# Feature-major query tiles in a linear-attention kernel: four instead of eight, with a new instruction order

## The chip, the cores and the metric

The kernel runs on one core of one Trainium2 chip. The metric is device time in microseconds of one execution. The core has five engines with a program of their own each: TensorE (matmuls, called PE in the profile), VectorE (DVE), ScalarE (ACT), GpSimd (POOL) and SyncE (SP), which here only issues DMA transfers. Engines wait for each other by semaphores.

## The reference

The input x has 2048 rows (tokens) of 512 features. Four layers change it in turn: attention A, feed-forward B, attention A and feed-forward B, each with the same weights in both of its places. Each layer normalizes x (layernorm without weights), computes, and adds its result to x.

```python
# A: linear attention, 32 heads of 16 features
q, k, v = split(layernorm(x) @ wqkv)
pq, pk = q @ w_phi, k @ w_phi                      # per head
phi_q = concat(softmax(pq), softmax(-pq))          # 32 features per head
phi_k = concat(softmax(pk), softmax(-pk))
kv, z = sum_s phi_k[s] v[s], sum_s phi_k[s]        # over all tokens
o = (phi_q @ kv) / (phi_q @ z + 1e-6)
x = x + o @ wo
# B: ReGLU feed-forward, 1376 hidden features
x = x + (relu(y @ W_gate) * (y @ W_up)) @ W_down   # y = layernorm(x)
```

## The kernel before, in words

The tokens are cut into 16 tiles of 128 rows. x stays in SBUF (`x_sb`) in bf16. Of each tile the kernel needs two layouts: tokens on partitions (for softmax sums and residuals) and features on partitions (as an operand of TensorE). The turn from one to the other is a transposing DMA on SP's queue (`dma_tr`, L443), or for tiles 0 and 1, in places where latency counts, a transpose on TensorE with a copy out of PSUM (`pe_tr`, L693).

At the start w_phi is multiplied into the key and query weights (`compose_k`, `compose_q`), so one projection gives pk or pq. The first attention is called A0, the first feed-forward B1, the second attention A2 and the second feed-forward B3; L0 to L3 are the layernorms ahead of them.

Keys and values: `kv_proj` and `kv_pair` project a tile, ScalarE takes the exponentials of pk and -pk, `knorm` (L741) sums them over each head's 16 features (Zk), takes the reciprocal (rZk) and scales (phik, on GpSimd or VectorE). `kv_acc` adds the tile to the sums kv and z in PSUM banks 0 and 1. When all 16 tiles are in, `kv_fin` (L792) copies the sums, masked to blocks, into `kvbd` (68 columns per group of heads) and, in A0 alone, into `kvf` (144 columns, L808).

Queries are done in one of two ways.

- Token-major: `q_proj` (L816) projects a tile with tokens on partitions; ScalarE takes the two exponentials (L827, L831). `qnorm` (L843) does on VectorE the sums Zq (L847) and the reciprocal rZq (L851), then on VectorE or GpSimd the ratio rho (L852), and in two halves the scaling phiq (L855), each half followed by a transposing DMA on SP into `qT` (qtr, L858). `num` (L915) multiplies the transposed tile by `kvbd` in eight matmuls of 68 columns (L921). VectorE divides: rden (L927) and o (L928). `qT` has four buffers.
- Feature-major: `q_fm` (L861) projects four tiles at once with features on partitions, so no transposing DMA is needed. `num_fm` (L874) multiplies the exponentials, not normalized, by `kvf` in eight matmuls of 144 columns (L886); eight of the columns give each softmax's own sum. Three copies take the result out of PSUM (numcp, L413 by way of `evac`, on ScalarE or VectorE), small operations put the two softmax sums together (zm L897, zd L900, zr L901, ab L902), VectorE scales (tsc, L906), and the two halves are added (o, L911, on VectorE or GpSimd). `kvf`, zm, ab and zd's neighbours lie in `qT` buffers 0 and 1, the results of numcp and tsc in tiles of `expk` that are no longer needed.

Both end in `out_proj` (L933): o is transposed (otr), multiplied by wo, and added to x (resid, L687). `center` (L700) then subtracts the mean (apply, L703), transposes the tile into `yT` (L1 tr, L697 or L708) and computes the scale (var L710, vx L712, rx L714).

In the kernel before, A0 has tiles 0 and 1 token-major, tiles 2 to 9 feature-major in two groups of four, and tiles 10 to 15 token-major. A2 is token-major throughout.

The feed-forward (`glu_up`, L947, `glu_down`, L1002) takes tiles 0, 1, then 2 and 3 together, then four at a time. For each of eleven pieces of the hidden features it computes gate and up in PSUM (L962), takes relu on ScalarE (L964) and the product on VectorE (h, L972 or L975). The last piece is short, done in token-major form (gu, L988) and transposed by DMA (htr, L995). `glu_down` multiplies by W_down (L1011).

The order of the work is not that of the calls. `emit` (L1026) emits some 3,960 operations, numbered in the order in which they are emitted. The table `ORDER` (L13) lists for each engine, as base-36 numbers, the operations in the order in which this engine runs them; a search done beforehand wrote it. `CHOICE` (L377) names the engine of each operation that two engines can do. `Program.schedule` replays the lists with assumed durations, and `prepare` derives the semaphore waits. An engine runs its list strictly in order, so a waiting instruction holds everything behind it in its list; on SP these are the transposing DMAs and the weight transfers.

Of the kernel before, what the change touches and what calls it, by code (L numbers as in the profile page):

```python
# [14 lines left out]
        "29 26 6 25 27 28 2a 2b 4t 2c 39 49 3u 4y 4e 44 5i 5n 58 5s 4j 6j 6k 67 73 72 8l 6d 84 6a 4o 83 8k 91 9x 9y 7r 96 9z c4 c5 9b c6 9g d9 da db b4 f9 f8 "  # L15
        "fm fl ay ee ef b2 eg gz gy fz h0 hx hw fy ij g5 g4 ik gb ga gg gh ii hv mk mj n4 n3 mu mt lm lq lt ne nd nn no nt r8 o5 o4 rf of op oq jv kn p0 pa pb "
        "vg pl pw pv vk q6 qg qh qr s1 ko sd sc sn xw xt sx sy t8 lg tt tj ti zn u4 ue u3 zu up uo uz wd wo wp x9 wz xa m8 ru ym yn xk z7 11o z8 yx 10k 11s zi "
        "10l 11v 10v 142 w2 12t yb 149 146 134 13p 135 13f 109 159 14z 13q 15a 15u 12a 15v 15k 14o 16x 178 177 17i 1b7 16m 18l 1aw 1c9 1db 1ad 1by 1d0 1e6 1dv "
        "1ea 1f0 1fg 1ew 1em 1gj 1fw 1gk 1fc 1gi 1jm 1hk 1hl 1hj 1kb 1fs 1ib 1ic 1kr 1l7 1g8 1ia 1j2 1j3 1gx 1ll 1lk 1j1 1m9 1ma 1nv 1k6 1ob 1mz 1my 1lj 1or "
        "1l3 1kn 1p7 1nn 1m8 1mn 1no 1mx 1pl 1pk 1ly 1q9 1nm 1o7 1nc 1qa 1pj 1qz 1qy 1on 1rq 1rp 1q8 1s4 1p3 1qx 1s3 1py 1ro 1t5 1t6 1s5 1s6 1t8 1qn 1t7 1u7 "  # L20
        "1ua 1u8 1xr 1uw 1uv 1u9 1xx 1y3 1uy 1ym 1yn 1ux 1z1 1z2 1y9 1yl 1zh 1zg 1z0 1zv 1zw 1zf 24t 1zu 24u 255 24v 24w 256 258 230 257 25u 25t 25h 25i 25k "
        "25w 25v 25j 26q 271 27d 272 22j 27n 27c 27z 27o 27y 289 28a 28l 28k 28v 28w 297 29h 296 29i 29t 29s 2be 23c 23x 2bp 2bq 24i 2cc 2cb 2c1 26f 2c0 2dj "
        "2cn 2cm 2di 2dt 2b3 2e5 2du 2e4 2ef 2eg 2er 2eq 2ft 2fu 2hu 2i5 2i6 2ih 2ig 2j2 2ir 2j3 2a7 2is 2d7 2kg 2k6 2kh 2k5 2l2 2l3 2ks 2kr 2mh 2le 2mg 2ld "
        "2fi 2hb 2ju 2m5 2qa 2pz 2qb 2n8 2ql 2qw 2qx 2qm 2sa 2r7 2sl 2sb 2r8 2ny 2sw 2sx 2t7 2sm 2pg 2t8 2um 2tj 2ti 2ul 2g8 2rz 2mv 2ua 2vw 2x5 2ak 2v0 2xg "
        "2xr 2xh 2od 2y3 2xs 2y2 2vd 2yd 2yp 2ye 2yo 2z0 2zb 2yz 2zm 2za 2zl 2gl 2wo 2zw 2zx 308 2wb 307 30z 2oq 31c 30m 322 "),
    "dve": (
        "2z 30 33 3a 3b 3e 3l 3m 3v 3k 3w 3p 2m 53 3z 5d 5x 5z 5t 5v 5u 60 5y 5w 7i 7g 7f 7h 6l 64 6m ao 74 ap 75 an am 85 7t 86 8m a0 7x 8n 7v a3 a1 a4 c7 ca "
        "c8 cb dc df b0 fa dg fn dd fo fb eh ek el ei em h1 h2 fq h4 hy hz h5 i1 il im i0 in io j2 j1 j3 j4 ix jd iz je iy j0 k6 jj k7 ku ky l1 l2 jo l3 l4 jp "
        "l6 l7 lv lw ju kc ly lz nu kh rc rg ki rh og ld ri o6 le or p1 rk pc pm rl vn vo q7 m5 px vq qi m6 xp qs kp s2 vs so se r4 sz xy xz t9 rr tk tu y1 u5 "
        "uf uq zr 13s we lh v0 zw zx zy zz rs vc 13t vz x0 wq w0 y8 y9 xb yo xl 13v 106 107 17w yy 15x zj 15y m9 z9 17x 15z 10m 17y 1b9 1ba 19o 10w 12u 11y 181 "  # L30
        "19p 14c 120 121 136 118 14d 13g 16c 14e 16d 150 19r 1cb 127 11k 13r 15b w3 128 1cc 18b 18c 15w 15l 1cd 14l 14m 16y 16j 16k 17j 179 17v 18i 18j 1a3 1a4 "
        "1bo 1bp 19b 1cq 1cr 18z 1aa 1ab 1b8 1dl 1ax 1dm 19n 1bv 1cx 1bw 1cy 1ca 1e8 1ds 1dt 1e7 1eb 1dc 1ey 1fe 1f3 1fh 1d1 1en 1ex 1jk 1kp 1fu 1fx 1gl 1fj "
        "1ft 12b 1k9 1fd 1l8 1ks 1gy 1dw 1hm 1g9 1hn 1j4 1j5 1gm 1id 1ha 1go 1nt 1l5 1nw 1mb 1ie 1i1 1hp 1mc 1la 1o9 1is 1k7 1jj 1p5 1oc 1gn 1os 1op 1ko 1p8 "
        "1lm 1ln 1n0 1ig 1n1 1n2 1l4 1lo 1pm 1lz 1lp 1nd 1np 1mo 1j7 1nq 1pn 1po 1r0 1pp 1r1 1o8 1r3 1qb 1qc 1s7 1s8 1oo 1p4 1rr 1rs 1se 1sf 1pz 1qo 1t9 1tg "
        "1rf 1xp 1ta 1th 1qe 201 1xs 1sw 1xv 202 203 20f 1xu 1ty 1tl 204 20g 1y1 208 209 1yo 1um 1y7 1y6 1yp 1z3 1ya 1yq 1z4 1yc 1zi 1zj 1zl 1zx 1zy 200 1zz "
        "20a 21r 21q 21s 21p 20d 221 222 227 22u 22v 22c 23n 23o 22d 20m 22i 248 249 235 236 265 23b 20n 2et 26r 266 2gm 2eu 24f 23u 23v 273 2ev 27e 2gn 280 "
        "28b 27p 2at 24g 2au 28m 2go 2lg 298 2cx 29j 28x 29u 2cy 2j5 26c 2j6 26d 2n9 2na 2f8 2f9 2bf 23d 2a6 2lh 2br 2aj 2li 2ll 2b0 2h1 2cd 2c2 2h2 2d4 2ff "
        "2co 23y 2b1 2or 2os 2dk 2nc 2d5 2fg 2e6 2eh 2dv 2es 2tl 2fv 2jk 2jl 2g7 2ra 2ou 2b4 2hv 2rb 2i7 2ow 2lv 2tm 2lw 2gk 2it 2h8 2h9 2ii 2j4 2no 2m2 2k7 "
        "2np 2rf 2m3 2jr 2js 2l4 2ki 2kt 2p6 2p7 2lf 2mi 2mu 2rp 2nv 2nw 2rq 2n7 2m6 2u0 2u1 2qc 2q0 2hc 2jv 2op 2oc 2vm 2pd 2qn 2qy 2pe 2r9 2sc 2rw 2rx 2vn "
        "2t9 2sn 2sy 2tk 2un 2uz 2u7 2u8 2vt 2vu 2vc 2x6 2xt 2ub 2xi 2wa 2yf 2wn 2y4 2yq 2s0 2zn 2z1 2zy 2zc 309 30l 30y 31b 31o 320 "),  # L40
    "pool": (
        "2p 0 1 4 2t 5 2w 2x 31 2 2u 2n 2o 32 3c 34 3d 3n 3o 2y 3x 3y 3f 2s 2r 2q 2v 61 62 66 63 69 6c 3 7j 7l 7k 7m 7n 7o 6n 7p 7q 76 ar aq as au at 87 av aw "
        "ax 8o a2 a5 c9 cc dh fp fc de fd ff ej h3 fs en h6 l5 lu lx rj jw vp jx vr vt xx kq y0 zv y2 100 13u 13x 17z li 11w rv 160 11x 14a 14b ma 162 19q 1bb "
        "1be 11z 10a yc 19t 14f 1bc yd 1cg rw w4 1ce 10b 18m 14p 1ec 16n 1ed 1f1 1f2 1fi 1fy 1fz 1jn 1kc 1kd 1bz 18n 16o 1ke 14q 1jo 1kt 1jp 1c0 1ku 1l9 1ae "
        "1ho 12c 1nx 1p9 1dx 1pa 1if 1od 1md 1ny 1oe 1ot 1j6 1d2 1ou 1me 1n3 1af 1r2 1nr 1ns 1sg 1sj 1s9 1sc 1rt 1qd 1sa 1tb 1te 1tc 1xt 206 1sh 1ti 1tj 20h "
        "1y4 1y5 20k 1xy 1xz 1y0 1ru 1yr 1yb 1z6 1z5 1zk 20i 20b 20o 20r 20p 2ew 2gr 2gp 22k 22l 2ey 2j7 2j8 23e 26g 2ja 24j 2nb 24k 23z 2lj 2ot 2b5 2tn 2to "
        "2tq 2d8 26h 2ne 2rc 2rd 2d9 2hd 2fj 2fk 2nz 2o0 2jw 2vx 2ph 2m7 2s1 2pi 2uc 2vy "),
    "pe": (
        "7 8 9 a b c d e f g h i j k 4p 4q 4r 4s l m n o p q r s t u v w x y z 35 36 37 38 10 11 12 13 14 15 16 17 3g 3h 3i 3j 18 45 46 47 48 3q 3r 3s 3t 4z 50 "
        "51 52 59 5a 5b 5c 4u 4v 4w 4x 4a 4b 4c 4d 40 41 42 43 5e 5f 5g 5h 4f 4g 4h 4i 5j 5k 5l 5m 19 1a 1b 54 55 56 57 1c 1d 1e 5o 5p 5q 5r 1f 1g 6f 6g 6h 6i "  # L50
        "1h 6y 6z 70 71 1i 1j 1k 1l 1m 1n 1o 8g 8h 8i 8j 1p 1q 1r 1s 6p 1t 1u 7z 80 81 82 1v 1w 6o 1x 1y 1z 20 21 22 23 24 4k 4l 4m 4n 9l 9m 9n 9o 8x 8y 8z 90 "
        "9h 9i 9j 9k 9p 9q 9r 9s 9t 9u 9v 9w 6q 6r 6s 6t 77 78 79 7a 92 93 94 95 bo bp bq br bs bt bu bv 6u 6v 6w 6x 97 98 99 9a 88 89 8a 8b bw bx by bz c0 c1 "
        "c2 c3 ct cu cv cw 9c 9d 9e 9f cx cy cz d0 d1 d2 d3 d4 d5 d6 d7 d8 f4 f5 f6 f7 fh fi fj fk 7b 7c 7d 7e 8c 8d 8e 8f 8p 8q 8r 8s dy dz e0 e1 a6 a7 a8 a9 "
        "e6 e7 e8 e9 e2 e3 e4 e5 ea eb ec ed fu fv fw fx ae af ag ah cd ce cf cg cl cm cn co 8t 8u 8v 8w aa ab ac ad gm gn go gp gi gj gk gl ai aj ak al ch ci "
        "cj ck gq gr gs gt gu gv gw gx di dj dk dl g0 g1 g2 g3 hn ho hp hq dq dr ds dt ia ib ic id cp cq cr cs dm dn do dp hr hs ht hu g6 g7 g8 g9 du dv dw dx "
        "es et eu ev eo ep eq er gc gd ge gf ie if ig ih mb mc md me mf mg mh mi f0 f1 f2 f3 ew ex ey ez h7 h8 h9 ha hf hg hh hi i2 i3 i4 i5 ip iq ir is hb hc "
        "hd he hj hk hl hm i6 i7 i8 i9 it iu iv iw j5 j6 j7 j8 j9 ja jb jc mz n0 n1 n2 mv mw mx my k2 k3 k4 k5 jf jg jh ji jy jz k0 k1 ml mm mn mo mp mq mr ms "
        "kr ks kt kv kw kx kz l0 jk jl jm jn lj lk ll ln n5 n6 n7 n8 lo lp lr ls n9 na nb nc nf ng nh ni nj nk nl nm jq jr js jt k8 k9 ka kb r5 r6 r7 r9 np nq "
        "nr ns kd ke kf kg ob oc od oe o0 o1 o2 o3 nw nx ny nz ra rb rd re o7 o8 o9 oa ol om on oo oh oi oj ok l9 la lb lc os ot ou ov kj kk kl km p6 p7 p8 p9 "
        "p2 p3 p4 p5 vd ve vf vh ow ox oy oz m1 m2 m3 m4 pr ps pt pu pd pe pf pg pn po pp pq ph pi pj pk vi vj vl vm py pz q0 q1 q8 q9 qa qb q2 q3 q4 q5 qc qd "  # L60
        "qe qf qj qk ql qm xm xn xo xq rx ry rz s0 qn qo qp qq qt qu qv qw qx qy qz r0 r1 r2 r3 s8 s9 sa sb s4 s5 s6 s7 sf sg sh si xr xs xu xv sj sk sl sm sp "
# [354 lines left out]
class Kernel:  # L416
# [609 lines left out]
    def emit(self):  # L1026
# [45 lines left out]
        for li in (0, 2):  # L1072
# [46 lines left out]
            if not last:  # L1119
                self.q_fm(F0 + 4, qring, A, 2)  # L1120
# [93 lines left out]
```

The softmax here doesn't subtract the row's maximum and nothing guards it: scores larger than these inputs give would overflow.

## Time and profile before

| | before |
|---|---|
| median of 3 runs | 379.43 us (379.27 to 379.86) |
| the profiled execution | 379.55 us timed, span 377.4 us |
| TensorE matmul busy | 367.7 us (97%), 2519 instructions |
| VectorE busy | 276.2 us (73%), 607 |
| ScalarE busy | 227.0 us (60%), 463 |
| GpSimd busy | 130.8 us (35%), 234 |
| granted TensorE clock | 1.000 |

The span is from the first to the last instruction of the profiled execution. Busy shares are averages over stages: keys and values of A0 last until about 53 us, B1 and the rest of A0's queries until about 150, B1 with A2's keys until about 236, and then come A2's queries and B3. A line of the groups reads: line of the kernel, engine, operation, output and inputs, shapes, count, then busy us and mean ns of one, then the idle time of the engine just before them and what ended it. A line of the timeline reads: start in us, duration, engine, line, operation, and in brackets how long the engine had been idle and what released it. Matmuls are pipelined, and their recorded durations overlap.

### The profile page before, as it was taken

What the parts mean: (1) busy time and instruction counts of PE and PEld (TensorE: products, weight loads), DVE (VectorE), ACT (ScalarE), POOL (GpSimd) and SP (SyncE); (2) the same over time, 40 slices, a digit from 0 to 9 for tenths busy, and PEclk for the clock granted to TensorE, in tenths of its full rate; (3) what the DMA queues carried; (4) which work ended last, traced back from release to release, by engine and by line L of the source; (5) the groups of instructions that cost most, each with busy time, mean ns of one, the idle gap of its engine ahead of it and who ended that gap; (6) DMA issues with size and microseconds to landing.
All of it is one profiled execution on the core that took longest, in us unless ns stands there. A gap on an engine that the chain in (4) does not pass through costs nothing.

```text
span 377.4 us, 6882 instructions
## 1 busy us (share of the span) xinstructions
PE 367.7 (97%) x2519; PEld 203.9 (54%) x2565; DVE 276.2 (73%) x607; ACT 227.0 (60%) x463; POOL 130.8 (35%) x234
## 2 busy tenths in 40 slices
PE   6999999999999999999999999999999999999997
PEld 5654555877744454454444446577664454445443
DVE  5999998989968676459799999898984654342323
ACT  3999878765744127874677568584635451653450
POOL 6799941133344001350463577023221201000020
PEclk9999999999999999999999999999999999999999
DMA  7632794313326444310300045335543442142012
GB/s 233 173 76 52 187 240 149 77 33 56 78 43 94 97 64 84 70 30 14 70 2 1 2 81 95 79 63 95 83 83 75 81 86 56 28 71 70 30 42 70
DMA packets 87856, 29.33 MB, mean 78 GB/s; under 512 B 79792, under 2 KB 86800, under 8 KB 87824
## 3 DMA queue, kind: packets, MB, share of 16 engines
q1 hardware_dynamic: 84368, 25.86, 33.7%
q10 hardware_dynamic: 3456, 3.05, 2.5%
q8 instruction: 20, 0.33, 0.4%
q14 instruction: 12, 0.10, 0.1%
HBM read 7.91 MB, written 2.10 MB: 27 GB/s over the span
## 4 chain that ended last, share of the span: by engine, by line
PE 85%; POOL 7%; DVE 3%; issue 2%; ACT 1%; DMA 1%; POOLq 0%; DVEq 0%
PE ps L962 37%; PE ps L1011 20%; PE ps L725 7%; PE ps L942 7%; POOL expk L750 5%; PE ps L822 5%; PE ps L988 3%; PE ps L921 2%; PE ps L787 1%; PE ps L886 1%; DMA hT<-in_A_wqkv_dram 1%; DVE Zk L744 1%; POOL rstd L648 1%; PE ps L868 1%; PE ps L539 0%
## 5 line engine op out<-in xcount | busy, mean ns | idle before, releaser
L962 PE MATMUL ps<-yT,Wgu 128*128 128x512 bf16 (+2 forms) x870 | 150.8, 320 | 0.6
L962 PEld LDWEIGHTS ps<-yT,Wgu 128*128 128x128 bf16 x880 | 78.5, 98 | 58.8 <-ACT expk L970 1.0
L964 ACT ACTIVATE gate_sb<-ps 128x512 bf16<-128x512 f32 (+2 forms) x110 | 50.7, 480 | 55.1 <-PE ps L962 41.8
L1011 PE MATMUL ps<-Wd,hT 128*128 128x512 bf16 (+4 forms) x354 | 79.3, 373 | 0.5
L1011 PEld LDWEIGHTS ps<-Wd,hT 128*128 128x128 bf16 (+1 forms) x363 | 34.6, 98 | 39.5 <-DVE hT L972 0.7
L972 DVE TENSOR_TENSOR hT<-gate_sb,expk 128x512 bf16<-128x512 bf16 (+2 forms) x70 | 23.9, 361 | 30.4 <-ACT expk L970 21.4
L970 ACT ACTIVATE expk<-ps 128x512 bf16<-128x512 f32 (+2 forms) x70 | 32.0, 475 | 22.2 <-PE ps L962 19.5
L710 ACT ACTIVATE sq<-x_sb,nmr 128x512 bf16<-128x512 bf16 x48 | 34.6, 721 | 10.3 <-DVE x_sb L687 6.6
L744 DVE TENSOR_REDUCE Zk<-expk 128x64 f32<-128x1024 bf16 x32 | 38.1, 1203 | 1.0 <-ACT expk L737 0.7
L714 POOL TENSOR_TENSOR rstd<-rv,mone 128x1 f32<-128x1 f32 x32 | 18.6, 589 | 50.2 <-DVE rv L712 50.0
L1013 DVE SCALAR_TENSOR_TENSOR x_sb<-ps,rstd,x_sb 128x512 bf16<-128x512 f32 (+2 forms) x33 | 23.9, 728 | 16.1 <-PE ps L1011 13.5
L942 PE MATMUL ps<-wo_p,oT 128*128 128x512 bf16 x118 | 30.8, 379 | 0.6 <-DVE oT L413 0.3
L975 DVE TENSOR_TENSOR hT<-gate_sb,ps 128x512 bf16<-128x512 bf16 (+2 forms) x40 | 21.7, 544 | 12.6 <-ACT gate_sb L964 6.4
L855 POOL TENSOR_TENSOR expq<-expq,rho 128x256 bf16<-128x256 bf16 x36 | 22.2, 624 | 24.4 <-DVE rho L852 23.7
L847 DVE TENSOR_REDUCE Zq<-expq 128x64 f32<-128x1024 bf16 x24 | 28.8, 1204 | 0.8 <-POOL rho L852 0.5
L687 DVE SCALAR_TENSOR_TENSOR x_sb<-ps,x_sb 128x512 bf16<-128x512 f32 x32 | 21.9, 687 | 8.6 <-PE ps L942 7.8
L750 POOL TENSOR_TENSOR expk<-expk,rZk 128x1024 bf16<-128x1024 bf16 x13 | 25.9, 2005 | 0.6 <-DVE rZk L746 0.6
L755 POOL TENSOR_TENSOR expk<-expk,rZk 128x512 bf16<-128x512 bf16 x17 | 19.1, 1134 | 11.8 <-DVE rZk L746 11.5
L822 PE MATMUL ps<-Wqp,yT 128*128 128x512 bf16 x91 | 22.8, 379 | 0.3
L725 PE MATMUL ps<-Wkp,yT 128*128 128x512 bf16 x84 | 22.0, 379 | 0.2
L725 PE MATMUL ps<-wv_p,yT 128*128 128x512 bf16 x85 | 21.9, 379 | 0.2
L712 POOL TENSOR_SCALAR rv<-rv 128x1 f32<-128x1 f32 x22 | 4.3, 203 | 45.3 <-ACT sq L710 45.3
(126 smaller groups left out, 514.1 us busy)
## 6 DMA issues: line engine op xcount, KB each, us to landing
out_dram<-x_sb ACTq DMA_DIRECT2D x15, 128.0 KB, 1.7
x_sb<-in_A_x_dram SPq DMA_DIRECT2D x3, 512.0 KB, 5.0
Wgu<-in_B_W_up_dram SPq DMA_DIRECT2D x4, 344.0 KB, 5.5
Wgu<-in_B_W_gate_dram SPq DMA_DIRECT2D x4, 344.0 KB, 4.3
Wd<-in_B_W_down_dram SPq DMA_DIRECT2D x5, 256.0 KB, 3.3
yT<-ytile SPq DMA_TRANSPOSE x56, 2.5
qT<-expq SPq DMA_TRANSPOSE x40, 2.5
x_sb<-in_A_x_dram SPq DMA_DIRECT2D x4, 128.0 KB, 3.6
```

The lines of the kernel that those rows point to most:

```text
L710: op("act", lambda e: e.activation(k.sq[:], k.x_sb[:, t, :], ACT.Square, scale=-float(D), bias=k.nmr[:, t, :], accum_out=k.rv1[:, t, :]), ...
L725: op("pe", (lambda ic, bank, W: lambda e: e.matmul(k.pb[bank][:], k.yT[:, ic, t * 128:(t + 1) * 128], W[:, ic, :], start=(ic == 0), stop=( ...
L744: op("dve", lambda e: e.tensor_reduce(k.Zk[:, zb, :], k.expk[:, t, :, :, :].rearrange("p g s (h f) -> p (g s h) f", f=16), AX.X, ALU.add), ...
L750: op("pool", lambda e: e.tensor_tensor(kv, kv, k.rZk[:, rb, :].unsqueeze(2).to_broadcast([P, 64, 16]), ALU.mult), [r("expk", t, 0), r("exp ...
L822: op("pe", (lambda ic, bank, tt: lambda e: e.matmul(k.pb[bank][:], k.yT[:, ic, tt * 128:(tt + 1) * 128], k.Wqp[:, ic, :], start=(ic == 0), ...
L847: op("dve", lambda e: e.tensor_reduce(k.Zq[:, b, :], k.expq[:, t, :, :, :].rearrange("p g s (h f) -> p (g s h) f", f=16), AX.X, ALU.add), ...
L942: op("pe", (lambda c, bank: lambda e: e.matmul(k.pb[bank][:], k.oT[:, ob, c, :], k.wo_p[:, c, :], start=(c == 0), stop=(c == NC - 1)))(c, ...
L962: op("pe", (lambda bank, W, ic, fc, Mf: lambda e: e.matmul(k.pb[bank][0:Mf, 0:n], W[:, ic, fc * 128:fc * 128 + Mf], k.yT[:, ic, c0:c0 + n] ...
L964: op("act", (lambda Mf, gb, gs: lambda e: e.activation(k.gate_sb[0:Mf, gs, 0:n], k.pb[gb][0:Mf, 0:n], ACT.Relu))(Mf, gb, gs), [self.RP[gb] ...
L970: op("act", (lambda Mf, ub, up: lambda e: e.activation(up[0:Mf, 0:n], k.pb[ub][0:Mf, 0:n], ACT.Copy))(Mf, ub, up), [self.RP[ub]], ru, 170 ...
L972: op("dve", (lambda Mf, up, gs, u: lambda e: e.tensor_tensor(k.hT[0:Mf, u, 0:n], k.gate_sb[0:Mf, gs, 0:n], up[0:Mf, 0:n], ALU.mult))(Mf, u ...
L1011: op("pe", (lambda fc, Kf, u, c0, bank, m0, m1: lambda e: e.matmul(k.pb[bank][:, m0:m1], k.hT[0:Kf, u, c0:c0 + 128], k.Wd[0:Kf, fc, m0:m1] ...
```

## The change

In A0 only tiles 2 to 5 are feature-major; tiles 6 to 9 become token-major like 10 to 15. The constant F1 = 6 marks the first tile after the feature-major ones; `N` uses it to decide whether a tile goes to `num_fm` or `num`, and from which tile on `qnorm` is called one tile ahead. The second `q_fm` call goes, and `q_proj` runs over the pairs from tile 6 on. The activation table's assumed duration in the planner and the alternatives that the planner knows for L0's centring change as well. ORDER and CHOICE are replaced by those of a new search, for all engines and the whole kernel.

```diff
 F0 = 2
+F1 = F0 + 4
...
-        op("act", ... ACT.Exp), [r("ones")], [r("sq"), r("tbl")], 1450, "table")
+        op("act", ... ACT.Exp), [r("ones")], [r("sq"), r("tbl")], 250, "table")
...
-            self.op2("act" if on_act else "dve", apply, dep, dst, {"dve": 407, "act": 825}, f"{tag} apply {t}", 250.0)
+            how = CHOICE.get(f"{tag} apply {t}", "act" if on_act else "dve")
+            other = "act" if how == "dve" else "pool" if t < 9 and how == "act" else "dve" if how == "act" else "act"
+            dd = {"dve": 407, "act": 825, "pool": 2090}
+            self.op2(how, apply, dep, dst, {e: dd[e] for e in (how, other)}, f"{tag} apply {t}", 250.0)
...
-        tb = (t + 2) % 4 if tag == "A0" and t < F0 else t % 4
+        tb = (t + 2) % 4 if tag == "A0" and (t < F0 or F1 % 4 == 2 and False) else t % 4
...
-                    if (F0 + 7 if li == 0 else 7) <= t < NT - 1:
+                    if (F1 - 1 if li == 0 else 7) <= t < NT - 1:
                         self.qnorm(t + 1, A)
-                    if li == 0 and F0 <= t < F0 + 8:
+                    if li == 0 and F0 <= t < F1:
                         self.num_fm(t, nring, wring, A)
...
-            if not last:
-                self.q_fm(F0 + 4, qring, A, 2)
-            for t in range(F0 + 8 if li == 0 else 8, NT, 2):
+            for t in range(F1 if li == 0 else 8, NT, 2):
                 self.q_proj([t, t + 1] if t < NT - 1 else [t], qring, A, last)
```

In the new lists, as far as the stages around the change go: at the start ScalarE copies yT of tile 1 before that of tile 2 and the V of tile 0, tile 0's copy goes to VectorE, and VectorE centres tile 1 behind the statistics of tiles 2 and 3. GpSimd takes the rstd of tiles 8 to 11 before the first phik. Behind `kv_fin` VectorE copies numerator 2 before oT of tile 0, and does Zq of tile 6 before it scales tile 2. On SP the query transposes stand so: otr 2, a weight, otr 3, htr 0, qtr 6 (two), otr 4, L1 tr 2 and 3, otr 5, qtr 7 (two), htr 1, otr 6, otr 7, L1 tr 5 and 4, qtr 8 (two), L1 tr 6 and 7, htr 2, qtr 9 (two), qtr 12, 11 and 10 (one half each), otr 8. Of the eight phiq of tiles 6 to 9, VectorE does 6 1, 7 0, 9 0 and 9 1, GpSimd the others. Zm, zd, o and numcp of tiles 2 to 5 are divided anew between VectorE, ScalarE and GpSimd.

## The prediction

> **What bounds the kernel now.** I read four views in this order: busy time by stretch, the timeline of the places where TensorE pauses, the timeline of the two matmul forms that the change exchanges, and the groups by line. The first view decides most. Its columns are the stretch in us, its length, then busy time with the number of instructions for TensorE matmuls, weight loads, VectorE, ScalarE and GpSimd, and the granted clock, DMA share and GB/s.
>
> ```profile
> 0.00:20.00 20.00, 16.47 (x149) 11.48 (x152) 15.05 (x34) 13.28 (x23) 14.93 (x45) 1.00 0.68 197
> 20.00:52.00 32.00, 31.73 (x236) 16.37 (x240) 31.73 (x45) 30.36 (x45) 30.83 (x29) 1.00 0.59 119
> 52.00:67.00 15.00, 13.81 (x129) 8.04 (x128) 13.16 (x31) 10.99 (x15) 1.50 (x3) 1.00 0.58 186
> 67.00:110.00 43.00, 42.63 (x410) 31.16 (x415) 36.43 (x103) 26.86 (x84) 13.86 (x31) 1.00 0.27 56
> 110.00:220.00 110.00, 109.42 (x560) 51.87 (x570) 85.52 (x175) 63.86 (x124) 37.44 (x65) 1.00 0.28 50
> 220.00:247.00 27.00, 26.48 (x259) 14.88 (x261) 24.48 (x52) 19.89 (x36) 12.35 (x19) 1.00 0.43 83
> 247.00:372.00 125.00, 124.21 (x766) 68.26 (x780) 68.14 (x170) 61.78 (x141) 19.88 (x43) 1.00 0.33 64
> ```
>
> Busy matmul time overlaps itself and proves little, so I priced the work by the interval at which matmuls follow each other in dense places: 216 ns for 512 columns (47 in 10 us in the dense feed-forward), 109 for 256, 83 for 192, 56 for 128, 62.5 for 144, about 32 for 68. Counting the weight loads of each stretch by form, TensorE's own work is 31.6 of the 32 us from 20 to 52, 12.6 of 15 from 52 to 67, 43.0 of 43, 109.8 of 110, 25.8 of 27, and 125 of 125. TensorE idles only in the start (about 10 us, filled with warm-up matmuls), 2.4 us between 52 and 67, 1.2 us between 220 and 247, and at the tail. Elsewhere a nanosecond taken from TensorE is a nanosecond of span, and a wait put ahead of a matmul in its program order is one too. From 20 to 52 VectorE is as full (31.7 of 32).
>
> The pauses of the second kind, on VectorE (first fence) and TensorE (second), around the change from keys and values to queries:
>
> ```profile
> 57.62 0.69 DVE L928 TENSOR_TENSOR osb<-ps,rden 128x512 bf16<-128x512 f32 x1
> 59.10 1.49 DVE L413 CAST expk<-ps 128x432 bf16<-128x432 f32 x3 [0.79 <-PE ps L886]
> 62.58 1.23 DVE L906 TENSOR_TENSOR expk<-expk,qT 128x1024 bf16<-128x1024 bf16 x1 [0.25 <-POOL qT L902]
> 65.14 0.43 DVE L413 COPY yT<-ps 128x512 bf16<-128x512 bf16 x1 [0.38 <-PE ps L697]
> ```
>
> ```profile
> 59.77 0.30 PE L886 MATMUL ps<-qT,expq 128*128 128x144 bf16 x2 [0.52 <-DVE expk L413]
> 65.72 0.64 PE L988 MATMUL ps<-Wgu,yT 128*128 128x192 bf16 x4
> ```
>
> The feed-forward starts at 65.72, as soon as VectorE has copied yT of tile 0 out of PSUM (65.14). This copy is the gate of the stage.
>
> **What the Trainium skill says.** "TensorE: Matmul & The Clock Gate", Back-to-back issue gap, gives N/2.4 + 2.5 ns for an isolated gap and about 81 ns sustained at 128 columns with weight loads. Only the first agrees here: four 144-column matmuls take 0.25 us (77.89 to 78.14, 62.5 each; the formula gives 62.5), eight of 68 columns 0.25 us (243.82 to 244.07, 31 each; 30.8).
>
> ```profile
> 77.89 0.41 PE L886 MATMUL ps<-qT,expq 128*128 128x144 bf16 x4
> 78.14 1.28 PE L962 MATMUL ps<-yT,Wgu 128*128 128x128 bf16 x20
> 243.82 0.42 PE L921 MATMUL ps<-kvbd,qT 128*128 128x68 bf16 x8
> 244.07 1.02 PE L822 MATMUL ps<-Wqp,yT 128*128 128x512 bf16 x4
> ```
>
> "Perfetto Trace Analysis", Identifying the Most-Contended Engine, warns that matmul busy share is no measure; the trace agrees (97% busy, yet 10 us of it warm-up and gaps at the start). "DMA: Bandwidth & Descriptors", DMA Transpose (X-bar), lets only the SP and ACT queues carry plain transposes, so each added one is a turn of SP here; the trace shows 1.19 to 1.27 us per issue and 2.5 us to landing.
>
> **The change part by part.** Edits that emit nothing new cost 0: the activation table's assumed duration, the second-choice engine of the centring (the engines chosen are those of before), the q_buf condition that ends in `and False`. Tiles 6 to 9 leave the feature-major path. TensorE's projection is the same: 16 matmuls of 512 columns and four exponentials of 1.02 us on ScalarE, in the same places and PSUM banks.
>
> Numerator. 32 matmuls of 144 columns become 32 of 68: 32 x (62.5 - 31) = 1.0 us less TensorE work, all in the full stretch after 67. It counts whole.
>
> Vector-like work. The rows:
>
> ```profile
> L847 DVE TENSOR_REDUCE Zq<-expq 128x64 f32<-128x1024 bf16 x24 | 28.8, 1204 | 0.8 <-POOL rho L852 0.5 <-ACT expq L827 0.2
> L906 DVE TENSOR_TENSOR expk<-expk,qT 128x1024 bf16<-128x1024 bf16 x8 | 9.7, 1213 | 2.6 <-POOL qT L902 2.6
> L928 DVE TENSOR_TENSOR osb<-ps,rden 128x512 bf16<-128x512 f32 x24 | 16.5, 687 | 0.9 <-DMA oT<-osb 0.2
> L413 ACT ACTIVATE expk<-ps 128x432 bf16<-128x432 f32 x11 | 5.9, 535 | 1.6 <-PE ps L886 1.6
> L855 POOL TENSOR_TENSOR expq<-expq,rho 128x256 bf16<-128x256 bf16 x36 | 22.2, 624 | 24.4 <-DVE rho L852 23.7
> ```
>
> A tile loses tsc (1.21) and zr (0.35) on VectorE and gains Zq 1.20, rZq 0.34, rden 0.35 and o 0.69: 1.0 us more, 4.1 for four. It loses three PSUM copies (0.41 to 0.60, ten of the twelve on ScalarE). The choice table then moves pieces both ways: four of eight phiq onto VectorE (0.47 each), two copies of tiles 4 and 5 and most zm, zd and o off it. I read the order lists of both versions by operation (the numbers are emission indices; 20 operations replace 20 at the projection, seven are added at tile 5, seven fewer stand at tile 9) and added the durations of everything that VectorE does from the end of kv_fin to the last product of feed-forward tiles 2 and 3: 49.3 us before, 48.9 after. So no extra load, and before had idle time there (13.2 of 15 us, 36.4 of 43). ScalarE loses 4 us and GpSimd about 3; both hidden, ScalarE having 16 us free of 43.
>
> DMAs. Eight more transposes on SP, 8 x 1.2 = 10 us. From 64 to 108 SP issues 18 transposes and a weight in 44 us (22 us busy), so there is room; what matters is who stands behind them, below.
>
> Start. The ScalarE order now has tile 1's yT copy first, and tile 1's centring goes behind the statistics of tiles 2 and 3. These statistics end at 8.43; two aggregates and the centring end near 8.95, the PE transposes near 9.3, then copy 1, copy 2 and V copy 0 at 0.5 to 0.6 each put the first key-weight copy at 10.9 instead of 10.43. The old order idles 0.27 behind it, the next V copy is then at 11.4 against 11.29, and the chain is gapless to the first key exponential (15.01). With an rstd power moved ahead of the first key product on GpSimd (1.02, given back behind it) I take +0.15 us; bounds -0.3 (VectorE idles no more than 0.3 of 32 us afterwards) and +0.5 (nothing absorbed). The weight transfers come in a new order, but the last gate and up pieces keep their place behind the same number of issues: 0.
>
> Turn at 52 to 67. VectorE's sum from kv_fin to the gate copy goes from 10.2 to 10.8: Zq 6 (1.20) enters, zm 2 and zd 2 and 3 (0.6) leave for GpSimd. Followed instance by instance from 56.95, the rden of tile 1: o 1 ends 57.9, numerator copy 0 runs 59.1 to 59.6, then oT copy, copies 1 and 2 to 60.95, Zq 6 to 62.15, zr, residual, tsc, o and centring to 65.0, PE transposes, gate copy at 65.4 instead of 65.14. Price +0.2; bounds 0 and +0.6.
>
> Tile 7. From the gate copy, VectorE has 36 instructions of 15.8 us up to phiq 7 0, which overlap by about 0.08 each: 12.9 us without a pause. Two SP issues follow (the second starts 1.25 later) and 2.5 to landing: 16.7. TensorE reaches the second half of num 7 after 17.0 us of its own work. Margin 0.3; with the share that VectorE idles from 67 to 88 now (1.9 of 21 us, 9%) it would be 0.9 late. Behind qtr 7 on SP stand the padding transpose of tile 1's feed-forward and the outputs of tiles 6 and 7, behind num 7 everything on TensorE. I take +0.25, since part of that idling is waiting for TensorE itself and moves with it; bounds 0 and +2. The transposes of tiles 8 and 9 also wait until tile 5's tsc has left qT buffers 0 and 1 (kvf, zm, ab lie there); SP gets to them four yT and oT transposes later, so 0. For the tiles after it the TensorE work between producer and consumer stays near that of before (wo 7 to its feed-forward 7.3 against 6.4 us, wo 11 5.0 against 6.5): 0, upper bound +0.5.
>
> Second attention. Choices and order change, not the work. At its turn the last key exponential (ends 233.13) releases Zk (233.16) and depends on TensorE's order, which holds the same matmuls ahead of it: 0, bounds -0.4 and +0.4. The tail is the same.
>
> Sum: -1.0 + 0.15 + 0.2 + 0.25 = -0.4 us on the profiled span of 377.4, whose own run was timed at 379.55; the median is 379.43 (379.27 to 379.86). Forecast 379.0.
>
> **The rivals.**
> A, the forecast, net -0.1 to -0.9: 378.5 to 379.3.
> B, the whole saving arrives: start and turn hide their delays, and the new order also takes a little of the 2.4 us or the 1.2 us. -0.9 to -1.7, say 378.1. For it: all TensorE stretches after 67 are full, so 1.0 is certain. Against: I find nothing that shortens the gate.
> C, slower: the query transposes of tile 7 land late. Each us that VectorE loses before phiq 7 0 is a us of TensorE. It decides from 1.4 us of lateness (0.76 + 1.0 less the 0.35 of start and turn); the 0.9 above plus one more SP turn of 1.2 ahead of qtr 7 is 2.1. That gives -1.0 + 0.35 + 2.1 = +1.4, about 380.8; 380.3 at 1.6.
> D, the saving doesn't exist: 68-column matmuls limited by the 98 ns weight load. The 31 ns spacing speaks against it. Same as before, 379.4.
>
> **How the numbers follow.** Measurement tells changes over 0.2%, 0.76 us, apart. A 0.45 (0.10 of it beyond -0.76), B 0.28, C 0.22, D 0.05. Faster 0.10 + 0.28 = 0.38, same 0.35 + 0.05 = 0.40, slower 0.22. The range holds A, D, most of B and half of C: 377.8 to 380.6; A's own range is 378.5 to 379.3.
>
> **What would show it.** 32 fewer 144-column and 32 more 68-column matmuls, eight more transposes; ScalarE's first key exponential near 15.2; the first feed-forward matmul near 66.1; TensorE's work in the 43 us after it about 1.0 us more advanced; a wait of num (L921) on a DMA into qT near 82 would speak for C. A changed pause between 220 and 247, or the gate copy earlier than 65, would make the prediction wrong.

## The result, and the profile after

| | before | after |
|---|---|---|
| median | 379.44 us (379.27 to 379.86, 4 runs) | 384.26 us (384.02 to 384.94, 4 runs) |
| ratio | | 1.0128, 95% interval 1.0111 to 1.0146 |
| span of the profiled execution | 377.4 us | 382.5 us |
| TensorE / VectorE / ScalarE / GpSimd busy | 367.7 / 276.2 / 227.0 / 130.8 us | 371.6 / 277.8 / 223.8 / 127.3 us |
| granted clock | 1.000 | 1.000 |

The change makes the kernel 4.8 us slower; the forecast was 379.0 us in a range of 377.8 to 380.6. The stretches again, now of the changed kernel (the last one is 5 us longer):

```profile
0.00:20.00 20.00, 16.87 (x149) 11.35 (x150) 14.69 (x33) 12.55 (x22) 14.87 (x45) 1.00 0.71 194
20.00:52.00 32.00, 32.00 (x237) 16.38 (x234) 31.10 (x43) 30.76 (x46) 29.83 (x28) 1.00 0.64 126
52.00:67.00 15.00, 13.07 (x125) 7.52 (x124) 13.21 (x30) 9.25 (x12) 3.18 (x8) 1.00 0.55 164
67.00:110.00 43.00, 42.71 (x417) 30.20 (x413) 40.55 (x107) 23.14 (x72) 12.76 (x29) 1.00 0.45 82
110.00:220.00 110.00, 108.68 (x578) 51.20 (x577) 79.29 (x169) 64.57 (x127) 36.50 (x62) 1.00 0.26 49
220.00:247.00 27.00, 26.69 (x249) 14.53 (x248) 24.38 (x53) 19.30 (x35) 12.18 (x20) 1.00 0.42 80
247.00:377.00 130.00, 129.39 (x810) 69.85 (x807) 73.00 (x181) 64.25 (x145) 18.04 (x40) 1.00 0.35 67
```

TensorE looks nearly as full as before, and the kernel is 5 us longer. Its busy time falls by 0.7 us in two rows (52 to 67, from 13.81; 110 to 220, from 109.42), which shows little of the loss. Its larger sum (371.6 against 367.7 us) is no growth in work: the trace of the kernel before lacks 46 of its 2565 matmuls. VectorE went from 36.4 to 40.6 of the 43 us after 67. The groups show the intended change: 32 matmuls of 144 columns in place of 64, 192 of 68 columns in place of 160, four more Zq, four fewer tsc.

```profile
L926 PE MATMUL ps<-kvbd,qT 128*128 128x68 bf16 x192 | 11.9, 194 | 1.0 <-DVE kvbd L802 0.5 <-DVE osb L933 0.4
L891 PE MATMUL ps<-qT,expq 128*128 128x144 bf16 x32 | 3.5, 226 | 0.3 <-DVE expk L415 0.3
L852 DVE TENSOR_REDUCE Zq<-expq 128x64 f32<-128x1024 bf16 x28 | 33.6, 1205 | 0.8 <-ACT expq L832 0.7
L911 DVE TENSOR_TENSOR expk<-expk,qT 128x1024 bf16<-128x1024 bf16 x4 | 4.9, 1217 | 0.0
```

The turn from keys to queries, VectorE and then TensorE:

```profile
58.91 0.69 DVE L933 TENSOR_TENSOR osb<-ps,rden 128x512 bf16<-128x512 f32 x1
60.56 0.61 DVE L415 CAST expk<-ps 128x432 bf16<-128x432 f32 x1 [0.96 <-PE ps L891]
64.23 1.22 DVE L911 TENSOR_TENSOR expk<-expk,qT 128x1024 bf16<-128x1024 bf16 x1
66.88 0.42 DVE L415 COPY yT<-ps 128x512 bf16<-128x512 bf16 x1 [0.42 <-PE ps L702]
```

```profile
53.43 0.30 PE L792 MATMUL ps<-vsb,expk 128*128 128x68 bf16 x4 [0.25 <-DVE expk L760]
54.12 0.81 PE L792 MATMUL ps<-vsb,expk 128*128 128x68 bf16 x20 [0.39 <-DVE expk L760]
67.45 0.62 PE L993 MATMUL ps<-Wgu,yT 128*128 128x192 bf16 x4
```

The gate copy stands at 66.88 (65.14 before), the first feed-forward matmul at 67.45 (65.72 before). TensorE was already late when it came here: it waits twice for scaled keys (expk), which it did not do before.

**Where the 5.1 us arise.** I laid the two traces side by side, matmul by matmul, and subtracted from each start the priced work ahead of it (the prediction's intervals: 216 ns for 512 columns, and so on). What is left is idle time. Its growth against the kernel before, at matmuls that both have:

| place | TensorE idles more by |
|---|---|
| start, to the second key product (14 us) | 0.57 |
| end of keys and values, to the numerators of tile 3 (60 us) | 1.17 |
| first feed-forward, 66 to 91 us | 0.88 |
| ahead of wo of tile 9 (120 us) | 1.49 |
| second attention up to its last key (247 us) | 0.0 |
| second feed-forward, 310 to 345 us | 0.97 |
| work saved: 32 fewer matmuls of 144 columns, 32 more of 68 | -0.96 |
| last matmul to the end of the span (2.69 before, 3.54 after) | 0.85 |
| sum | 5.0, of 5.1 |

The third view is the chain of work that ended last. Columns: start, us, what.

```profile
115.37 1.25 SPq L863
116.67 1.26 SPq L863
117.98 4.13 DMA oT<-osb
...
312.73 3.96 DMA yT<-ytile
...
336.55 2.31 SPq L1000
338.90 3.02 DMA oT<-osb
```

Three times the chain leaves TensorE for a transpose that lands 3.0 to 4.1 us after its issue, while the median is 2.5. The first is the output of tile 9. VectorE ends it at 109.44 (o, 108.76 + 0.68); SP issues its transpose at 117.98, 8.5 us later, since six others stand ahead of it from 109.65 on, with one pause of 0.5 us at 114.9:

```profile
104.49 3.81 SPq L863 DMA_TRANSPOSE qT<-expq  x3
108.34 1.27 SPq L944 DMA_TRANSPOSE oT<-osb  x1
109.65 3.90 SPq L863 DMA_TRANSPOSE qT<-expq  x3
113.59 1.27 SPq L1000 DMA_TRANSPOSE hT<-h10t  x1
115.37 2.56 SPq L863 DMA_TRANSPOSE qT<-expq  x2
117.98 1.26 SPq L944 DMA_TRANSPOSE oT<-osb  x1
```

The kernel before reaches this place with as little to spare. There o of tile 9 ends at 113.62. Its transpose, the second of the two in this line, is issued at 114.64 and lands at 117.14, 0.24 us ahead of its first matmul:

```profile
113.33 2.57 SPq L939 DMA_TRANSPOSE oT<-osb  x2
```

### The profile page after: what moved, and what is told of

It is laid out like the page before. It is cut to its first block, busy times and chain, and to the rows that moved or that the text cites. A ratio compares the mean times of both kernels' runs of the same rounds, so it can differ in the third digit from the quotient of the medians.

```text
span 382.5 us, 6921 instructions
## 1 busy us (share of the span) xinstructions
PE 371.6 (97%) x2565; PEld 202.4 (53%) x2565; DVE 277.8 (73%) x612; ACT 223.8 (59%) x455; POOL 127.3 (33%) x229
## 4 chain that ended last, share of the span: by engine, by line
PE 83%; DVE 8%; DMA 4%; ACT 2%; SPq 2%; issue 1%; POOL 0%; DVEq 0%
PE ps L967 34%; PE ps L1016 18%; PE ps L730 9%; PE ps L947 7%; PE ps L827 5%; PE ps L993 3%; DVE Zk L749 2%; PE ps L771 2%; DMA oT<-osb 2%; PE ps L926 2%; PE ps L792 1%; DMA x_sb<-in_A_x_dram 1%; DMA yT<-ytile 1%; DVE rZk L751 1%; DVE expk L760 1%
## 5 line engine op out<-in xcount | busy, mean ns | idle before, releaser
L967 PEld LDWEIGHTS ps<-yT,Wgu 128*128 128x128 bf16 x880 | 77.3, 98 | 61.1 <-ACT expk L975 3.1
L1016 PE MATMUL ps<-Wd,hT 128*128 128x512 bf16 (+3 forms) x363 | 80.0, 373 | 0.0
L947 PE MATMUL ps<-wo_p,oT 128*128 128x512 bf16 x128 | 32.4, 379 | 1.9 <-DMA oT<-osb 1.5
L852 DVE TENSOR_REDUCE Zq<-expq 128x64 f32<-128x1024 bf16 x28 | 33.6, 1205 | 0.8 <-ACT expq L832 0.7
L719 POOL TENSOR_TENSOR rstd<-rv,mone 128x1 f32<-128x1 f32 x32 | 17.5, 555 | 42.3 <-DVE rv L717 41.6
L760 POOL TENSOR_TENSOR expk<-expk,rZk 128x512 bf16<-128x512 bf16 x21 | 23.4, 1129 | 14.3 <-DVE rZk L751 14.1
L827 PE MATMUL ps<-Wqp,yT 128*128 128x512 bf16 x112 | 27.4, 379 | 0.0
L719 POOL TENSOR_TENSOR rstd<-rv,mhalf 128x1 f32<-128x1 f32 x16 | 9.0, 566 | 47.2 <-DVE rv L717 46.8
L857 POOL TENSOR_TENSOR rho<-rZq,Zq 128x32 f32<-128x32 f32 x17 | 4.8, 287 | 56.3 <-DVE rZq L856 42.1
```

The lines of the kernel that those rows point to most:

```text
L719: op("pool", lambda e: e.tensor_tensor(k.rstd[:, t, :], k.rv1[:, t, :], pw, ALU.pow), [r("rv1", t), r("mone"), r("mhalf")], [r("rstd", t)] ...
L760: self.op2("dve" if t >= NT - 2 and u else "pool", (lambda kv, u: lambda e: e.tensor_tensor(kv, kv, k.rZk[:, rb, u * 32:u * 32 + 32].unsqu ...
L827: op("pe", (lambda ic, bank, tt: lambda e: e.matmul(k.pb[bank][:], k.yT[:, ic, tt * 128:(tt + 1) * 128], k.Wqp[:, ic, :], start=(ic == 0), ...
L852: op("dve", lambda e: e.tensor_reduce(k.Zq[:, b, :], k.expq[:, t, :, :, :].rearrange("p g s (h f) -> p (g s h) f", f=16), AX.X, ALU.add), ...
L947: op("pe", (lambda c, bank: lambda e: e.matmul(k.pb[bank][:], k.oT[:, ob, c, :], k.wo_p[:, c, :], start=(c == 0), stop=(c == NC - 1)))(c, ...
L967: op("pe", (lambda bank, W, ic, fc, Mf: lambda e: e.matmul(k.pb[bank][0:Mf, 0:n], W[:, ic, fc * 128:fc * 128 + Mf], k.yT[:, ic, c0:c0 + n] ...
```

## The experiments

Theory O: the time is lost in places of the new lists and can be mended place by place. Theory F, the rival: the token-major form itself makes VectorE and SP's queue too full, so that a mended place hands its time to the next. Each group of runs is compared with the kernel before on the same chip (its medians there: 379.50, 379.50, 379.67 and 379.55 us). Ratios are to that.

**Undoing parts of the new lists.**

```diff
 e1: all lists    +the kernel before's order and engines for what it starts before 36 us
 e2: sp           +otr 9, qtr 14 (first half), qtr 12 (second half), -otr 9, otr 10, ...
 e3: all lists    +the kernel before's order and engines for what starts after 250 us
 e4: e1 + e2 + e3
```

e1: 

> The changed kernel, but every operation that the kernel before starts in the first 36 us of its trace stands in the order, and on the engine, that it had there; all else is the changed kernel's list. Theory O (the lost time sits in places of the new lists, not in the token-major form): the 0.57 us that TensorE loses in the first 14 us and the 1.17 us at the end of the keys and values (TensorE waits there for the last scaled keys, VectorE runs without a pause from 32 us on and starts that stretch 0.6 us late) both go: -1.7 us, 382.6 us. Theory F (the form makes VectorE and SP's queue too full, so a mended place hands its time to the next wait): -0.6 at most, 383.7 us or more.

e2: 

> The changed kernel with one operation moved in SP's list: the output transpose of tile 9 goes ahead of two query transposes (tile 14 first half, tile 12 second half), 2.6 us earlier. TensorE's wait of 1.5 us ahead of wo of tile 9 should go. Theory O: -1.5 us, 382.8 us. Theory F: SP's queue is full from 104 to 121 us, so the two query transposes behind it or the next outputs come late instead: -0.5 us or less, 383.8 us or more.

e3: 

> The changed kernel up to 250 us of its trace; what starts later stands in the order, and on the engines, of the kernel before. The computation there is the same in both kernels. Theory O: the 1.0 us that TensorE loses more than before between 310 and 345 us (the yT of tile 11 and the outputs of tile 14 come late) goes: -1.0 us, 383.2 us. Theory F: nothing of the first attention reaches this far, so also -1.0; if instead the later start of this stage were the cause, no change.

e4: 

> The three edits before together (first 36 us, output transpose of tile 9, everything from 250 us on). Theory O: they add, -4.2 us, 380.1 us; what is left above the kernel before is the 0.9 us lost between 60 and 91 us, less the 1.0 us that the narrower numerators save. Theory F: 382.5 us or more.

| run | median us | ratio (95% interval) |
|---|---|---|
| e1 | 382.71 | 1.0090 (1.0075 to 1.0105) |
| e2 | 382.23 | 1.0077 (1.0062 to 1.0093) |
| e3 | 383.37 | 1.0106 (1.0089 to 1.0122) |
| e4 | 380.30 | 1.0024 (1.0015 to 1.0033) |

All four came out as theory O had it, within 0.6 us. The waits went where they were meant to go: e2 has none left for oT between 100 and 130 us, e3 none between 250 and 345. They nearly add: 1.6, 2.0 and 0.9 apart (4.5 in sum), 4.0 together. Theory F is wrong for these three places. In e4 one loss against the kernel before stood out on TensorE: 0.95 us between 66 and 84 us. Its waits there, of the weight loads, are those of the changed kernel:

```profile
PEld ps L967 <- DVE hT L980: 0.5, 2, 0.3
PEld ps L967 <- ACT gate_sb L969: 0.4, 1, 0.4
```

A gate or up product waits for a PSUM bank that has still to be read, by VectorE's h or ScalarE's relu. Each pause ahead of a matmul of the changed kernel can be put down to the last reader of the PSUM bank that it writes: 0.40 us behind h, 0.16 behind a residual, 0.24 behind o of tile 6 and 0.06 behind a relu. So nearly all of it is VectorE reading late.

**The start, the centring, and lists of another kind.**

```diff
 e7: all lists  +the kernel before's order and engines for what it starts before 13 us
 e6: dve        Zk 8, Zk 9, -L0 apply 13, rZk 8, Zq 0, +L0 apply 13, rZk 9, ...
 e5, e12: new form (F1 = F0 + 4), from e4; lists rearranged at 52 to 132 us (e5), then at 40 to 140 (e12)
 e8: old form, from the kernel before; lists rearranged at 40 to 140 us in the same way
 e10, e11: e5 and e8 rearranged further, from the start to 255 us
```

e7: 

> The changed kernel with the kernel before's order and engines only for what that one starts in its first 13 us. If the new start list costs what the two first profiles differ by (TensorE 0.57 us more idle at the second key product): -0.6 us, 383.7 us. If that difference is the scatter of the first loads (it was between 0.3 and 0.6 us in three runs with the same start list, and 0.75 and -0.3 in two with the old one): no change, 384.2 us, and what the run of the first 36 us gained came from the order behind the start.

e6: 

> The changed kernel with one VectorE instruction moved: the centring of tile 13 (1.69 us in the trace, 0.96 before, 0.34 where GpSimd is idle) goes behind the softmax sum Zq of tile 0, where GpSimd's run of three phik has ended. Theory O with a VectorE-bound turn: VectorE runs without a pause from there to the end of the keys, so what it saves (about 1.2 us less the 0.3 that tile 13 comes later) reaches TensorE's wait for the last scaled keys: -0.8 us, 383.4 us. If that wait came from the late start alone: no change, 384.2 us.

e5: 

> Four feature-major tiles, the lists of the run with the three edits, and its lists between 52 and 132 us rearranged by a local search over the planner's replay with random delays (VectorE, ScalarE and GpSimd instructions up to some tens of ns longer, one transpose in eight 1.6 us late), so that work does not stand close behind its producer. Theory O (the lost time is a matter of the lists): the 0.95 us that TensorE still loses between 66 and 84 us goes for the most part: -0.8 us from 380.3, 379.5 or less, equal to the kernel before or faster. Theory F (VectorE has too much to do there with token-major tiles): 380.2 us or more.

e8: 

> Control: the kernel before, eight feature-major tiles, its lists between 40 and 140 us rearranged by the same local search with the same delays. Theory O: the old form gains little, since TensorE loses nothing there: 379.2 us (-0.3), so that the new form with searched lists is at least as fast. Theory F: the old form keeps 0.7 us or more ahead of the new form with searched lists.

e12: 

> Four feature-major tiles; the lists of the first searched run, searched on between 40 and 140 us alone. A second sample of how much the time scatters between lists that the replay holds equal. Theory O: 379.0 us; theory F: 379.6 us.

e10: 

> Four feature-major tiles; the lists of the first searched run, searched on in the same way from the start to 255 us. Theory O: with lists as good as the old form's the 1.0 us of narrower numerators shows: 378.9 us, at or below the old form searched as far. Theory F (token-major tiles cost about as much in waits as the narrower numerators save, wherever the lists put them): 379.5 us, 0.5 above the old form searched as far.

e11: 

> Control: eight feature-major tiles; the lists of the searched old form, searched on in the same way from the start to 255 us. Both theories: 378.9 us, within 0.3 of the first searched old form; what counts is its distance to the new form searched as far.

| run | form | median us | ratio (95% interval) |
|---|---|---|---|
| e7 | new | 383.37 | 1.0102 (1.0088 to 1.0115) |
| e6 | new | 384.79 | 1.0143 (1.0129 to 1.0157) |
| e5 | new | 379.54 | 1.0006 (0.9998 to 1.0014) |
| e12 | new | 379.60 | 0.9995 (0.9987 to 1.0003) |
| e8 | old | 379.01 | 0.9985 (0.9975 to 0.9996) |
| e10 | new | 382.74 | 1.0079 (1.0067 to 1.0092) |
| e11 | old | 381.25 | 1.0039 (1.0025 to 1.0053) |

e7: the start list alone costs about 0.9 us, and e1 shows some 0.7 more from the order between 13 and 36 us. In traces the start scatters: TensorE's idle time up to the second key product was 0.26 to 0.63 above the kernel before in five runs with the new start list, and -0.43 to +0.75 in others with the old one; so the 0.57 of the table is right only on average.

e6 is a miss, and tells something. VectorE did reach the centring of tile 13 after Zq 0, but GpSimd was no longer idle: rZk 8, now earlier, had let it begin the next phik. VectorE and GpSimd in e6:

```profile
37.16 2.04 DVE L670 TENSOR_SCALAR ytile<-x_sb,rstd,nmr 128x512 bf16<-128x512 bf16 x1
```

```profile
31.46 7.59 POOL L760 TENSOR_TENSOR expk<-expk,rZk 128x1024 bf16<-128x1024 bf16 x4
```

The centring ends at 39.20, GpSimd's run of four phik at 39.05. In the changed kernel it took 1.69 and ended at 37.25, GpSimd's run at 37.11. "SBUF — State Buffer" of the Trainium skill, section SBUF: two separate sides, calls the port pair that the two share an exclusive lock, held for a whole instruction; this trace agrees. VectorE is 0.4 us later right behind this centring and 0.9 later when it copies the sums (`kvbd`, 55.41 against 54.50). TensorE is 1.0 later at the first numerators, with tile 13's late transpose as a second cause: the run doesn't separate the two. Nor does it show what the centring alone is worth.

e5 and e12 take the 0.95 us between 66 and 84 away (0.2 and none are left), with tiles 6 to 9 token-major. So this too was a matter of the lists. e5 took the 379.5 us that theory O gave for it, e12 the 379.6 that theory F gave. e10 and e11 are misses: in their profiled executions the rearranged start lost 2.0 and 3.0 us on TensorE up to the second key product (e11's is the slowest of its five executions). That the assumed durations of the first loads are to blame is likely, but not shown.

Yet e5 and e12 stop at the time of the kernel before, and half a us above e8; theory F gave 0.7. By these runs alone theory F would have held: the narrower numerators' 1.0 us did not show. The next two groups say why.

**The instruction fetches.** SP's transposes take 1.19 to 1.27 us to issue, but a few take 1.9 to 2.4. Each of these nine in the changed kernel has an instruction fetch of 16 KB beside it. The DMA view of the changed kernel from 119.9 to 121.1 us has one, while the output transposes of tile 9 and 10 are under way:

```profile
q8 instruction: 1, 0.02, 5.7%
```

There are 20 of these on the whole page, about one per 128 matmuls with their weight loads (2565 / 20). Shifting them should tell whether they matter.

```diff
-NWARM = 70
+NWARM = 46      # the last 24 warm-up matmuls leave PE's list
```

e9: 

> The changed kernel without the last 24 of the 70 warm-up matmuls (their results are not used; they run at 16 to 19 us, where TensorE waits anyway); all lists are otherwise as they were. In the changed kernel's trace an instruction fetch of 16 KB begins every 126 matmuls or so, and each of the three transposes for which TensorE waits (tile 9's outputs at 120 us, tile 11's yT at 314, tile 14's outputs at 340) is issued beside such a fetch. 24 matmuls less put each fetch about a fifth of a period later, 4 to 5 us there. If the fetch makes these transposes late: the three waits (1.5, 0.6 and 0.3 us more than before) go or shrink, -1.5 us or more, 382.7 us or less, unless the fetch meets another one that matters. If SP's full queue alone makes them late: no change, 384.2 us.

e9 took 382.00 us, ratio 1.0056 (1.0044 to 1.0069): 2.3 us less from leaving out matmuls that nothing waited for. The outputs' landing times (min/median/max) between 112 and 124 us, changed kernel and e9:

```profile
DMA to landing us min/median/max: 3.3/3.7/4.1
```

```profile
DMA to landing us min/median/max: 2.5/2.5/2.5
```

The fetch begins at 122.5 in e9 and not at 120.0, and falls on a query transpose (4.4 us to landing) that TensorE needs later. The wait ahead of wo 9 is gone, and so are those at 314 and 340. The three make up 2.4 of the 2.6 us by which the two profiled spans differ.

The full queue and the fetch act together. With 2.5 us to landing, tile 9's output would have landed at 120.48, and TensorE came there at 120.68: a lead of 0.2 us by this estimate, where o itself had been ready 11 us ahead. The queue used up that time. In the kernel before the lead was 0.24 us, but its fetch, at 118.3, falls on the query transposes behind this output (4.1 us to landing), and nobody waits for those. In e2, with more lead, the fetch falls on a query transpose as well. So SP's full queue left no lead and the fetch made the wait; on which transpose a fetch falls is partly chance.

**The closing waits.** From the last matmul to the end of the span every run of the new form up to here took 3.52 to 3.59 us, every one of the old form 2.69 or 2.70, whatever its lists. The last data lands equally soon in all (1.81 to 1.83 us after the last weight load). The difference is in SP's closing waits (`final_dma_waits`), before and after:

```profile
L345 SPq EVENT_SEMAPHORE  x24: 17/28/111, 375.4 to 376.9; - x24
```

```profile
L346 SPq EVENT_SEMAPHORE  x24: 17/28/593, 379.6 to 382.0; - x24
```

The kernel gives its DMAs 48 semaphores in turn and waits for all at the end, in index order, two to an instruction. 195 DMAs put the last stores on semaphores 1 and 2; eight more transposes, 203, put them on 9 and 10. The built program joins the waits from the middle outwards: semaphore 2 is waited for in the 23rd of 24 instructions, semaphore 10 in the 15th, and nine more follow it at 60 to 70 ns each, with a gap of 0.4 us among them.

```diff
-        for s, c in self.final_counts.items():
-            if isinstance(s, tuple) and c:
-                eng.wait_ge(dma_sems[s[1]], 16 * c)
+        first = sum(o.is_dma for o in self.ops) % self.n_dma_sems
+        for j in range(self.n_dma_sems):
+            i = (first + j) % self.n_dma_sems
+            if self.final_counts["d", i]:
+                eng.wait_ge(dma_sems[i], 16 * self.final_counts["d", i])
```

e13, this alone in the changed kernel: 

> The changed kernel, but SP's closing waits on the DMA semaphores begin behind the last one used, so that the last stores' semaphores are waited for last. No other instruction changes. If the order of these waits makes the end longer: -0.85 us, 383.4 us, and 2.7 us from the last matmul to the end in place of 3.5. If the longer end comes from the last store itself: no change, 384.2 us.

e14, in e12: 

> Four feature-major tiles, the lists searched on between 40 and 140 us, and the closing waits in the order of e13. Theory O with this term: 0.85 us under the 379.6 of these lists, 378.75 us: the narrower numerators' 1.0 us shows, less what TensorE still idles. If the token-major form had another cost: 379.4 us or more.

e15, in e8: 

> Control: eight feature-major tiles, the first searched lists of the old form, closing waits in the order of e13. The last stores' semaphores are the 23rd of 24 waits already: -0.05 us, no change that can be measured, 379.0 us.

e16, in e4: 

> The run with the three edits of the lists (380.3 us), closing waits in the order of e13: -0.85 us, 379.45 us, the time of the kernel before. The 0.95 us that TensorE still loses between 66 and 84 us then stands against the 0.96 that the narrower numerators save.

| run | form | median us | ratio (95% interval) |
|---|---|---|---|
| e13 | new | 383.32 | 1.0097 (1.0083 to 1.0111) |
| e14 | new | 378.70 | 0.9978 (0.9970 to 0.9986) |
| e15 | old | 379.06 | 0.9986 (0.9980 to 0.9993) |
| e16 | new | 379.58 | 1.0003 (0.9995 to 1.0011) |

All four as expected, within 0.15 us. e13's waits, none of which blocks any longer:

```profile
L348 SPq EVENT_SEMAPHORE  x24: 17/28/28, 379.5 to 381.2; - x24
```

In the profiles the end takes 2.96 to 3.02 us in these new forms (2.7 was expected for e13), so 0.55 of the 0.85 came back there; the medians moved by 0.7 to 0.9. What makes up the difference is not known. e14 is faster than both kernels, by 0.22% against the kernel before. Against the old form with lists of the same kind (e15) it is 0.36 us ahead; the two intervals overlap, so that is not settled.

The closing waits are thus most of what hid the narrower numerators' 1.0 us in the searched lists. The rest is again waits on transposes that land late beside a fetch: 0.3 us at 101 us in e5, 0.6 at 144 us in e12 and 0.5 there in e14. e8 and e15, with eight transposes fewer, lose nothing at these places. Whether still better lists avoid this is open; theory F is wrong for the larger losses, and these small ones could still be the form's own.

## Why the prediction was wrong, point by point

- **Numerators, -1.0.** Right. In the changed kernel's chain of work four 68-column matmuls take 0.13 us, 33 ns each, which also rules out rival D. The saving follows for every run of the new form from its count of matmuls; the losses elsewhere (6.0 us in the table) are six times as large.
- **"Edits that emit nothing new cost 0: the activation table's assumed duration", and the start at +0.15 (at most +0.5).** The start list costs about 0.9 us (e7). In the changed kernel's trace the table load takes 1.28 us, then 0.21 for the first activation; the planner now holds it to take 0.25. An assumed duration emits nothing, but it shapes the lists. That this figure is the cause of the start's loss is argued, not shown.
- **Turn, +0.2 (at most +0.6).** 1.2 us. I had put down VectorE as full from 20 to 52 us, and then added its load only from kv_fin on. What VectorE loses in that full stretch comes out undiminished at the last scaled keys: it is late there by 0.6 from the start and by 0.7 at one centring (1.69 us in place of 0.96). The part that I did price was right: kv_fin starts 1.4 us late (54.50 against 53.07), and from there to the gate's copy it takes 12.4 us in place of 12.1, +0.3. e1 shows what the first 36 us cost as a whole; the centring's own share was not separated.
- **Tile 7, +0.25 (rival C).** The term did not come: tile 7's last transpose landed at 85.14, 0.4 us ahead of its matmul at 85.53. The 0.9 us here were lost to PSUM banks that VectorE read late (h, a residual, an o), which I had not priced; the sum of VectorE's load was the wrong measure, because what counts is who stands ahead of each h.
- **"SP issues 18 transposes and a weight in 44 us, so there is room", and 0 for the tiles behind tile 7 (at most +0.5).** The step that failed most: it put the tiles behind tile 7 at nothing, and 1.5 us were lost ahead of wo of tile 9. The room is an average; from 104 to 121 us the queue is all but full, and tile 9's outputs stand 8.5 us in it. And each transpose was counted as 2.5 us to landing, while the trace of the kernel before has some at 4.1 and 4.4 beside a fetch (issued at 117.25 and 96.02). A lead of 0.2 us doesn't survive that. Rival C had a transpose late behind SP's queue, at the wrong tile and without the fetch, and its 380.8 us was far short as well.
- **Second attention, 0 (at most 0.4 either way).** Right up to 247 us, but I did not follow the lists into the second feed-forward, where 1.0 us went to two late transposes.
- **"The tail is the same."** Wrong by 0.85 us: I counted the eight DMAs as turns of SP and not as eight steps in a ring of semaphores.

Rivals A and B had the saving but not the losses. The range missed because three terms priced at nothing (lists behind 88 us, second feed-forward, tail) were worth 3.4 us together; the first was bounded at +0.5, the other two not at all.

## What to carry to other kernels

When a change comes with a new order for the whole program, price the order everywhere, and not just the edited stage: look for the producers that stand close ahead of their consumer in each queue, since a delay that the planner doesn't know turns each of them into a wait. A queue's room is read from its fullest 20 us, not from an average. Adding DMAs can move whatever is assigned to DMAs in turn, as far as the last wait of the program.

## What the runs showed of the hardware that I had not expected

- An instruction fetch of 16 KB, about one per 128 matmuls with weight loads, disturbs two transposing DMAs beside it. Between 50 and 345 us of the changed kernel the one under way when a fetch begins (12 cases) lands after 3.8 to 4.4 us in place of 2.5. The next, where it is issued within about 1 us (9 cases), takes 1.9 to 2.4 us to issue in place of 1.27 and lands after 3.2 to 3.6. The kernel before has these fetches too; there they fall on transposes that have lead enough.
- VectorE's 128x512 centring took 0.34 us alone and 0.96, 1.69 or 2.04 us beside a GpSimd phik, ending about 0.15 us behind the end of GpSimd's instruction in the two traces compared (39.20 and 39.05 in e6, 37.25 and 37.11 in the changed kernel).
- A wait on semaphores that are already complete costs SP about 60 ns (24 instructions in 1.5 us), and those that stand behind the last store's wait add to the time.
